# Products of the second half taken chunk by chunk for both column halves, the reciprocal moved by one pair, scratch buffers per batch, SBUF buffers at one common offset

## The chip, the cores and the metric

The program runs on one core of one Trainium2 chip. The metric is device time in microseconds (us); three timed runs of the kernel before gave 576.07 (median), 576.04 and 576.54. A separate, profiled execution gave the trace that is read below; it took 574.43 us, of which 572.6 us are the span from its first to its last instruction.

## The reference, cut to what matters

Attention over 4 batches x 8 heads (576 positions, 64 channels) with rotated q and k, then a gated unit with a mixing matrix over positions, then a causal convolution gate with two more matrix products:

```python
attn = softmax(rot(q) @ rot(k).T / 8) @ v                 # (4, 8, 576, 64), heads side by side: x (4, 576, 512)
h = gelu_tanh(x @ w_in)                                   # 512 -> 1024
u, v = h[..., :512], h[..., 512:]
v_n = (v - mean(v)) / sqrt(var(v) + 1e-6) * g_ln
v_s = einsum('ts,bsd->btd', w_sg, v_n) + b_sg
x2 = x + (u * v_s) @ w_out
gate = sigmoid(causal_conv5(x2, conv_w))
out = (gate * (x2 @ w_val)) @ w_out2                      # (4, 576, 512)
```

## The kernel before

The kernel records every operation as a task of a planner (`Plan`): an engine, an estimated cost, the keys it reads and writes. `P.order()` lays the tasks out once, by what they depend on and when they are due by those estimates, and the instructions are then written in that order. So each engine runs a fixed list, in order, and an instruction that waits holds up all that stands behind it on its engine. SyncE's list (SP) is nearly all DMA issues, about 350 rows.

**First half, attention.** It works on 16 pairs of heads (4 a batch), one pair after the other. A pair's phase on TensorE (`phase`) is a mix of score products of the next pair for its row maxima (`s_unit`, lines 527 and 535, each followed on VectorE by a maximum `mx` or `mn`, lines 529 and 537, that frees the PSUM buffer) and of this pair's transposed scores (`st_unit`, lines 577 and 585, freed by an exponential on ScalarE, line 590). Then comes the pair's "v stretch": the products with v (`pv_unit`, lines 608 and 618) and the row sums (`sum_unit`, line 644). Meanwhile VectorE turns and splits q and k of a later pair (`prep_high`, line 252) and converts a part of a weight (`job_v`, `wa_half`, lines 302 to 308).

A pair's row sums go their own way to memory. ScalarE copies them to `ss` (line 648), a DMA turns them into 128x9 in `rc` (line 651), VectorE takes the reciprocal (line 653), and a DMA writes it to `r_d` (line 654). The unscaled result goes to `xu_d` (line 626). Later the loads `xs<-xu_d` (line 745) and `rb<-r_d` (line 749, spread over 64 partitions) bring both back for GpSimd to multiply. The last 64 positions of two batches are gathered in `xr` and `rr` by `xr_load` (lines 772 and 777): one such call is three DMAs and covers one pair. Eight calls stand in the phases of pairs 8 to 15 (`job_loads`), eight more in the first batch of the second half.

**Second half.** `part_a(b)` makes, for each batch, units of 12 or 24 matmuls with 512 columns (x by the v half of w_in, line 803; the chunk c=4 is `xr`), four units of 24 with 288 columns (the u half, line 844) and four of 28 (the mixing product, `g_unit`, lines 858 and 861; the last chunk of positions, `t4`, comes in by line 861). After these come `x2_part` (line 927), `val_part` (line 960) and `out_part` (line 989). Every product is a sum over four chunks k of 128 rows and three terms: high x high, high x low, low x high (`three`). A unit owns one of four PSUM buffers, each of two banks, and its result is read as a whole when all its matmuls are done. Within the unit a loop over the two banks is the outer one: all 12 terms for the first column half (or the first 128 positions), then all 12 for the second.

The units' inputs come from the other engines: `vn` (the normalised v) is split into a rounded high part by ScalarE and a low part by GpSimd (line 253), chunk by chunk. The first instruction of the second half on ScalarE that uses memory of the first half, the Gelu of line 809 with its table load, waits until all that touched this memory is done, the DMA `r_d<-rc` of the last pair included.

Of the kernel before, what the change touches and what calls it, by code (L numbers as in the profile page):

```python
# [166 lines left out]
def mixer_kernel(ctx: ExitStack, tc: tile.TileContext, qk, v, vrem, cs, w_in, g_ln, w_sgT, b_sg,  # L167
# [32 lines left out]
    mark = const.tile([128, 1], F32, name="mark")  # L200

# [4 lines left out]
    RB = tiles(const, "rb", 2, [128, 4 + S], F32)  # L206

# [33 lines left out]
    ones_b = [att.tile([128, 32], F32, name=f"ones_b{h}") for h in range(2)]  # L241

# [355 lines left out]
    def pv_unit(i, us):  # L598
# [25 lines left out]
        def st(q):  # L624
            for hf in range(2):
                q.dma_start(out=xu_d[i][:, HALF * hf:HALF * hf + HALF].rearrange("(h d) c -> d h c", h=2),
                            in_=xu[64 * hf:64 * hf + 64])
        dma(290, st, [("xu", j2)], [("xu_d", i)], n=2)

    def sum_unit(i, ps, kps):  # L630
# [22 lines left out]
        add("DVE", 0.25, lambda: nc.vector.reciprocal(rc, rc), w=[("rc", j2)])  # L653
        dma(5, lambda q: q.dma_start(out=r_d[i].rearrange("(p c) -> p c", c=9), in_=rc), [("rc", j2)], [("r_d", i)])
# [10 lines left out]
    def attention():  # L665
# [45 lines left out]
        for i in range(NPAIR):  # L711
# [8 lines left out]
            rot = [P.last_pe]  # L720
            if i + 2 < NPAIR:
# [4 lines left out]
            sum_unit(i, PS[2], ("ps", 2))  # L726

# [11 lines left out]
    def three(n):  # L739

        return [(x, y) for x, y in ((0, 0), (0, 1), (1, 0))][:n]

    def x_load(b, hp, after=()):
        i, y = 4 * b + hp, hp % 2
        dma(290, lambda q: q.dma_start(out=XS[y][:, 4:], in_=xu_d[i]), [("xu_d", i)], [("xs", y)], after=after)

        def ld(q):
            for h in range(2):
                q.dma_start(out=RB[y][64 * h:64 * h + 64, 4:], in_=r_d[i][S * h:S * h + S].partition_broadcast(64))
# [19 lines left out]
    def xr_load(b, part, op=()):  # L769
        m, hp = part  # L770
        i, cc = 4 * (b + m) + hp, slice(64 * m, 64 * m + 64)
        dma(32, lambda q: q.dma_start(out=XR[1].bitcast(F32)[:, hp, cc], in_=xu_d[i][:, 512:576]), [("xu_d", i)],
            [("xr", m, hp)], [*op, *P.readers.get(("XR", "l"), ())])

        def ld(q):
            for h in range(2):
                q.dma_start(out=RR[64 * h:64 * h + 64, hp, cc], in_=r_d[i][S * h + 512:S * h + S].partition_broadcast(64))
        dma(32, ld, [("r_d", i)], [("rr", m, hp)], op, n=2)

    def xr_prep(b, after=()):  # L780

        def f():
            return XR[1].bitcast(F32)
        parts = [(m, hp) for m in range(2) for hp in range(4)]
        tt("P", lambda: RR, f, lambda: RR, ALU.mult, 512, [("xr", *x) for x in parts], [("rr", *x) for x in parts], after)
        keys = [("rr", *x) for x in parts]
        acopy(lambda: XR[0], lambda: RR, 512, keys, [("XR", "h")])
        tt("P", lambda: XR[1], lambda: RR, lambda: XR[0].bitcast(F32), ALU.subtract, 512, [("XR", "h"), *keys],
           [("XR", "l"), *[("xr", *x) for x in parts]])

    def part_a(b):
# [4 lines left out]
        for c0 in (0, 2, 4)[:3 - b % 2]:  # L796
            cs_ = (c0, c0 + 1) if c0 < 4 else (4,)

            def mm(ps, cs_=cs_):
                for y, c in enumerate(cs_):  # L800
                    for k in range(4):
                        for z, (p, q) in enumerate(three(3)):
                            nc.tensor.matmul(ps[:, y], X[p][:, k, 128 * c:128 * c + 128] if c < 4 else XR[p][:, k], Wm[q][:, k, 512:1024], start=k == z == 0,  # L803
                                             stop=k == 3 and z == 2)
# [31 lines left out]
        def u_unit(dd):  # L836
            dc = slice(128 * dd, 128 * dd + 128)

            def mm(ps):
                for hf in range(2):  # L840
                    cols = slice(HALF * hf, HALF * hf + HALF)
                    for k in range(4):
                        for z, (p, q) in enumerate(three(3)):
                            nc.tensor.matmul(ps[:, hf, 0:HALF], Wm[p][:, k, dc], X[q][:, k, cols], start=k == z == 0,  # L844
                                             stop=k == 3 and z == 2)
# [4 lines left out]
        def g_unit(dd):  # L850
            dc = slice(128 * dd, 128 * dd + 128)

            def mm(ps):
                for hf in range(2):
                    cols = slice(HALF * hf, HALF * hf + HALF)
                    for k in range(4):
                        for z, (p, q) in enumerate(three(3)):
                            nc.tensor.matmul(ps[:, hf, 0:HALF], VN()[p][:, k, dc], SG[q][:, k, cols], start=k == z == 0,  # L858
                                             stop=False)
# [15 lines left out]
        if b == 0:  # L875
            for x in range(8):
                xr_load(2, divmod(x, 4))
# [32 lines left out]
    def x2_part(b, dds=range(4)):  # L910
        j = b % 2
        for dd in dds:
# [9 lines left out]
            def mm(ps, dc=dc):  # L922
                for hf in range(2):
                    cols = slice(HALF * hf, HALF * hf + HALF)
                    for k in range(4):
                        for z, (p, q) in enumerate(three(3)):
                            nc.tensor.matmul(ps[:, hf, 0:HALF], w2("o", p)[:, k, dc], (T["gh"], T["gl_"])[q][j][:, k, cols],  # L927
                                             start=k == z == 0, stop=k == 3 and z == 2)
# [20 lines left out]
    def val_part(b):  # L949
        j = b % 2  # L950
        rc = slice(64 * j, 64 * j + 64)
        for dd in range(4):
            dc = slice(128 * dd, 128 * dd + 128)

            def mm(ps, dc=dc):
                for hf in range(2):
                    cols = slice(HALF * hf, HALF * hf + HALF)
                    for k in range(4):
# [174 lines left out]
```

## Time and profile before

| | |
|---|---|
| timed, median of 3 | 576.07 us |
| profiled execution | 574.43 us |
| its span, first to last instruction | 572.6 us |
| TensorE busy | 558.7 us, 98% |
| VectorE, ScalarE, GpSimd busy | 70%, 48%, 42% |
| DMA engines' mean share | 45% |

The profile gives busy time by engine, 40 slices of the span, a chain of work that ended last, and timelines by engine. Matmuls overlap one another, so that "busy" of TensorE says only that something was under way. What one matmul costs the stream is the distance from its start to that of the next; over a long run of one kind this is the run's length in the chain divided by its count. Granted clock is 1.00 (2.4 GHz) from 24 us on.

### The profile page before, as it was taken

The numbers are of one execution on the slowest core, as the hardware profiler recorded it, in microseconds if no ns is written. First come the engines' busy times: TensorE is split into PE (matmuls) and PEld (weight loads), VectorE is DVE, ScalarE is ACT, GpSimd is POOL, SyncE is SP. The second block draws the span as 40 slices with busy tenths as digits, with TensorE's granted clock in tenths as the row PEclk, the third lists the DMA queues.
The fourth block names the chain that finished last, engine by engine and source line by source line (L and its number), as shares of the span: only waits on it lengthen the run. The fifth ranks groups of instructions, "written<-read, shape, count | busy, mean of one in ns | idle before, by whom it ended". The sixth has DMA issues, their size and how long they took to land.

```text
span 572.6 us, 12028 instructions
## 1 busy us (share of the span) xinstructions
PE 558.7 (98%) x4658; PEld 466.5 (81%) x4658; DVE 400.8 (70%) x616; ACT 276.7 (48%) x448; POOL 241.3 (42%) x220
## 2 busy tenths in 40 slices
PE   6999999999999999999999999999999999999996
PEld 4677777777777776768999989989999999899985
DVE  4678888888888878534667866645779997647720
ACT  2457666666666666533614426315337443333311
POOL 5534545454545444642876778546410010121100
PEclk9699999999999999999999999999999999999999
DMA  5446747475655565475267481462423341210002
GB/s 211 127 125 191 192 128 204 137 190 130 183 164 150 172 193 153 117 196 138 54 187 259 141 285 58 140 183 73 164 79 112 119 137 42 78 56 1 38 37 92
DMA packets 58697, 77.84 MB, mean 136 GB/s; under 512 B 29968, under 2 KB 34576, under 8 KB 58640
## 3 DMA queue, kind: packets, MB, share of 16 engines
q1 hardware_dynamic: 58496, 77.08, 45.2%
q8 instruction: 36, 0.59, 0.4%
q14 instruction: 21, 0.17, 0.1%
q10 hardware_dynamic: 144, 0.00, 0.0%
HBM read 56.38 MB, written 18.95 MB: 132 GB/s over the span
## 4 chain that ended last, share of the span: by engine, by line
PE 80%; DVE 6%; DMA 6%; ACT 3%; POOL 2%; SPq 2%; issue 1%; POOLq 0%; ACTq 0%; DVEq 0%
PE ps L577 11%; PE ps L608 10%; PE ps L960 9%; PE ps L927 9%; PE ps L989 9%; PE ps L858 6%; PE ps L644 5%; PE ps L527 5%; PE ps L844 4%; PE ps L803 4%; PE ps L585 3%; PE ps L618 2%; PE ps L861 1%; DMA xs<-xu_d 1%; DVE raw L252 1%
## 5 line engine op out<-in xcount | busy, mean ns | idle before, releaser
L529 DVE TENSOR_REDUCE mx<-ps 128x2 f32<-128x576 f32 x128 | 91.4, 753 | 34.1 <-ACT e L590 18.8
L590 ACT ACTIVATE e<-ps 128x576 f32<-128x576 f32 x144 | 85.6, 652 | 30.5 <-PE ps L585 20.3
L608 PE MATMUL ps<-e,vm 128*64 128x288 f32 x512 | 65.6, 409 | 0.0
L858 PE MATMUL ps<-s_h,vn 128*128 128x288 f32 x256 | 56.3, 296 | 1.1 <-POOL vn L253 1.1
L608 PEld LDWEIGHTS ps<-e,vm 128*64 128x64 f32 x512 | 35.3, 137 | 24.7 <-issue 2.6
L253 POOL TENSOR_TENSOR ac<-e,e 128x576 f32<-128x576 f32 x32 | 45.0, 1427 | 7.0 <-ACT e L590 6.8
L252 DVE TENSOR_TENSOR raw<-raw,cst 128x1152 f32<-128x1152 f32 (+2 forms) x35 | 41.6, 1196 | 6.3 <-DMA cst<-cs 6.3
L527 PE MATMUL ps<-kh,qp 64*128 64x288 f32 x256 | 40.4, 346 | 4.1 <-ACT kh L256 1.8
L858 PEld LDWEIGHTS ps<-s_h,vn 128*128 128x128 f32 x256 | 42.8, 188 | 1.3 <-POOL vn L253 1.3
L527 PEld LDWEIGHTS ps<-kh,qp 64*128 64x128 f32 x256 | 23.3, 188 | 19.2 <-issue 8.2
L577 PE MATMUL ps<-mr,one_r 64*128 64x288 f32 x256 | 38.1, 291 | 0.3 <-DMA mr<-mn 0.3
L577 PE MATMUL ps<-qh,kh 64*128 64x288 f32 x256 | 38.2, 293 | 0.0
L577 PE MATMUL ps<-ql,kh 64*128 64x288 f32 x256 | 38.0, 292 | 0.0
L577 PE MATMUL ps<-qh,kl 64*128 64x288 f32 x256 | 38.0, 292 | 0.0
L960 PE MATMUL ps<-xh,wl_v 128*128 128x288 f32 x128 | 37.8, 296 | 0.0
L960 PE MATMUL ps<-xl,wh_v 128*128 128x288 f32 x128 | 37.8, 296 | 0.0
L960 PE MATMUL ps<-xh,wh_v 128*128 128x288 f32 x128 | 37.8, 295 | 0.0
L260 POOL COPY mark<-wf 1x1 f32<-1x1 f32 x12 | 2.1, 174 | 84.8 <-DVE wf L308 84.8
L844 PE MATMUL ps<-XH,w_l 128*128 128x288 f32 x128 | 37.7, 295 | 0.0
L858 PE MATMUL ps<-s_l,vn 128*128 128x288 f32 x128 | 37.7, 295 | 0.0
L844 PE MATMUL ps<-XL,w_h 128*128 128x288 f32 x128 | 37.7, 294 | 0.0
L844 PE MATMUL ps<-XH,w_h 128*128 128x288 f32 x128 | 37.7, 294 | 0.0
(168 smaller groups left out, 1590.0 us busy)
## 6 DMA issues: line engine op xcount, KB each, us to landing
raw<-qk SPq DMA_DIRECT2D x31, 576.0 KB
xu_d<-xu SPq DMA_DIRECT2D x32, 144.0 KB
rb<-r_d SPq DMA_DIRECT2D x32, 144.0 KB
xs<-xu_d SPq DMA_DIRECT2D x16, 288.0 KB
x_d<-xs SPq DMA_DIRECT2D x16, 288.0 KB
g_d<-vs SPq DMA_DIRECT2D x16, 288.0 KB
vm<-v SPq DMA_DIRECT2D x16, 256.0 KB
wr<-w_in SPq DMA_DIRECT2D x8, 512.0 KB
```

Source lines behind the costliest of these rows:

```text
L252: return add("DVE", dve(n), lambda: nc.vector.tensor_tensor(out_(), a(), b(), op), r, w, after, lock=True)
L253: return add("Pool", pool(n), lambda: nc.gpsimd.tensor_tensor(out_(), a(), b(), op), r, w, after, lock=True)
L527: nc.tensor.matmul(ps[:, h, 0:HALF], QP[j2][rows, c], kh[rows, cols], start=True, stop=True)
L529: add("DVE", 0.72, lambda: nc.vector.tensor_reduce(out=MX[j2][:, hk, :, c], in_=ps[:, :, 0:HALF], axis=AX.X, op=ALU.max), [kps], [("mx", j ...
L577: nc.tensor.matmul(ps[:, h, 0:HALF], x[rows, keys] if o < 3 else x[rows], y[rows, cols], start=o == 0, stop=o == 3)
L590: add("Act", 0.62, lambda: nc.scalar.activation(E[n], ps[:, :, 0:HALF], AF.Exp), [kps], [("e", n)])
L608: nc.tensor.matmul(pv[64 * hf:64 * hf + 64, h, 0:HALF], VM[j2][:, j, h], E[EU[i, us[hf]]][:, h], start=j == 0, stop=False, skip_group_chec ...
L844: nc.tensor.matmul(ps[:, hf, 0:HALF], Wm[p][:, k, dc], X[q][:, k, cols], start=k == z == 0, stop=k == 3 and z == 2)
L858: nc.tensor.matmul(ps[:, hf, 0:HALF], VN()[p][:, k, dc], SG[q][:, k, cols], start=k == z == 0, stop=False)
L927: nc.tensor.matmul(ps[:, hf, 0:HALF], w2("o", p)[:, k, dc], (T["gh"], T["gl_"])[q][j][:, k, cols], start=k == z == 0, stop=k == 3 and z == 2)
L960: nc.tensor.matmul(ps[:, hf, 0:HALF], w2("v", p)[:, k, dc], (T["xh2"], T["xl2"])[q][j][:, k, cols], start=k == z == 0, stop=k == 3 and z == 2)
L989: nc.tensor.matmul(ps[:, y], lhs, w2("q", q)[:, k], start=k == z == 0, stop=k == 3 and z == 2)
```

## The change

Five things are changed.

1. `product` replaces the loops of lines 803, 844, 858, 927, 960 and 989. The loop over the two banks (y) is now the innermost: each chunk and term is done for both column halves (or both blocks of 128 positions) before the next. The number of matmuls is the same. In the mixing product the four matmuls with `t4` come after all 24 others.
2. The reciprocal and the write to `r_d` leave `sum_unit` and become `sum_end`, called one pair later, with dependencies that place it after that pair's phase.
3. `xu_d` and `r_d` are one DRAM buffer a batch in place of one a pair, so that `xr_load` brings a batch's four pairs with three DMAs. There are four such calls (12 DMAs) where there were sixteen (48).
4. Three unused tiles (`pad0`, `pad1`, `pad2`) and the move of `mark` to the attention's pool shift the SBUF addresses. The start addresses in the two built programs, modulo 256 bytes:

| tiles | before | after |
|---|---|---|
| XH, XL | 128 | 224 |
| w_h, w_l, s_h, s_l, xr | 0 | 224 |
| vn, t4 | 32 | 224 |
| wh_o to wl_q, gh0, gl0 | 224 | 224 |
| xh2, xl2, yh, yl, yr | 0 | 224 |
| q, k, e and all others of the attention | 96 | 64 |

5. What follows from the planner: other orders on SP and a few exchanges on ScalarE and GpSimd near the end of the attention.

```diff
-    xu_d = [dram.tile([128, S], F32, name=f"xu_d{i}") for i in range(NPAIR)]
+    xu_d = [dram.tile([HP, 128, S], F32, name=f"xu_d{b}") for b in range(B)]
-    r_d = [dram.tile([2 * S], F32, name=f"r_d{i}") for i in range(NPAIR)]
+    r_d = [dram.tile([HP, 2 * S], F32, name=f"r_d{b}") for b in range(B)]
...
-        if i >= 8:
-            xr_load(0, divmod(i - 8, 4), [mq[i]])
+        if i in (8, 10):
+            xr_load(0, i // 2 - 4, [mq[i]])
...
         dma(5, rows, [("ss", 0)], [("rc", j2)])
-        add("DVE", 0.25, lambda: nc.vector.reciprocal(rc, rc), w=[("rc", j2)])
-        dma(5, lambda q: q.dma_start(out=r_d[i].rearrange("(p c) -> p c", c=9), in_=rc), [("rc", j2)], [("r_d", i)])
+
+    def sum_end(i, after=()):
+        rc = RC[i % 2]
+        add("DVE", 0.25, lambda: nc.vector.reciprocal(rc, rc), w=[("rc", i % 2)], after=after)
+        dma(5, lambda q: q.dma_start(out=r_d[i // HP][i % HP].rearrange("(p c) -> p c", c=9), in_=rc), [("rc", i % 2)], [("r_d", i)])
...
             rot = [P.last_pe]
+            if i:
+                sum_end(i - 1, [*rot, *P.writer.get(("mn", (i + 1) % 2, 1), ())] if i + 1 < NPAIR else ())
...
+        sum_end(NPAIR - 1)
...
-    def three(n):
-
-        return [(x, y) for x, y in ((0, 0), (0, 1), (1, 0))][:n]
+    def product(n, out_, lhs, rhs, ends=True):
+
+        terms = [(k, p, q) for k in range(4) for p, q in ((0, 0), (0, 1), (1, 0))]
+        for z, (k, p, q) in enumerate(terms):
+            for y in range(n):
+                nc.tensor.matmul(out_(y), lhs(p, k, y), rhs(q, k, y), start=not z, stop=ends and z == len(terms) - 1)
...
-                for hf in range(2):
-                    cols = slice(HALF * hf, HALF * hf + HALF)
-                    for k in range(4):
-                        for z, (p, q) in enumerate(three(3)):
-                            nc.tensor.matmul(ps[:, hf, 0:HALF], Wm[p][:, k, dc], X[q][:, k, cols], start=k == z == 0,
-                                             stop=k == 3 and z == 2)
+                product(2, lambda y: ps[:, y, 0:HALF], lambda p, k, y: Wm[p][:, k, dc], lambda q, k, y: halves_of(X[q][:, k], y))
...
+                product(2, lambda y: ps[:, y, 0:HALF], lambda p, k, y: VN()[p][:, k, dc], lambda q, k, y: halves_of(SG[q][:, k], y), False)
                 for hf in range(2):
                     cols = slice(HALF * hf, HALF * hf + HALF)
-                    for k in range(4):
-                        for z, (p, q) in enumerate(three(3)):
-                            nc.tensor.matmul(ps[:, hf, 0:HALF], VN()[p][:, k, dc], SG[q][:, k, cols], start=k == z == 0,
-                                             stop=False)
                     for z in range(2):
                         nc.tensor.matmul(ps[:, hf, 0:HALF], T4()[b % 2][:, dc], SG[z][:, 4, cols], start=False, stop=z == 1)
```

VectorE in the phase of pair 12 and the v stretch that follows, before (`mx` are the maxima that free the score buffers `ps`, `wf` the end of a weight's conversion):

```order
L529 TENSOR_REDUCE mx_177<-ps_121 128x2
L653 RECIPROCAL rc_199<-rc_199 128x9
L529 TENSOR_REDUCE mx_177<-ps_123 128x2
L529 TENSOR_REDUCE mx_177<-ps_124 128x2
L529 TENSOR_REDUCE mx_177<-ps_122 128x2
```

The same engine where the reciprocal stands now, at the end of the v stretch:

```order
L308 SCALAR_TENSOR_TENSOR wt_179<-wr_177,wt_179 128x256
L310 SCALAR_TENSOR_TENSOR wf_178<-wr_177,wt_179 128x256
L658 RECIPROCAL rc_175<-rc_175 128x9
L531 TENSOR_REDUCE mx_154<-ps_97 128x2
L531 TENSOR_REDUCE mx_154<-ps_98 128x2
```

The reciprocal has moved from between the fourth and the fifth maximum of a phase to ahead of the first, and it is now that of the pair before.

SP from the small weights to the last `r_d<-rc`, before (`rr<-r_d` are the calls of line 777, `cwr` the convolution's weights):

```order
L362 DMA cwr<-conv_w 128x40
L745 DMA xs_135<-xu_d_74 128x576
L777 DMA rr<-r_d_109 64x64 x2
L626 DMA xu_d_84<-xu_196 64x2x288 x2
L777 DMA rr<-r_d_110 64x64 x2
L651 DMA rc_199<-ss_197 128x1x9
L777 DMA rr<-r_d_111 64x64 x2
L777 DMA rr<-r_d_112 64x64 x2
L755 DMA x_d_89<-xs_134 128x576
L654 DMA r_d_116<-rc_199 128x9
```

SP at the same place now, from the last `xu_d` to the last `r_d<-rc`:

```order
L628 DMA xu_d_72<-xu_173 64x2x288 x2
L653 DMA rc_176<-ss_174 128x1x9
L769 DMA x_d_77<-xs_110 128x576
L763 DMA rb_112<-r_d_90 64x576 x2
L769 DMA x_d_78<-xs_111 128x576
L659 DMA r_d_92<-rc_176 128x9
```

The load of `cwr` is no longer in this piece: it now goes out ahead of the results and sums of the last pair but one (in before, after them). Between the last `rc<-ss` and the last `r_d<-rc` two `rb` loads stand in place of four `rr` loads; both stores of `xs` (`x_d<-xs`) must now be issued first.

## Rows read from the trace of the kernel before

**Rows 1.** The page's first part: busy us, share of span, instructions by engine.

```profile
PE 558.7 (98%) x4658; PEld 466.5 (81%) x4658; DVE 400.8 (70%) x616; ACT 276.7 (48%) x448; POOL 241.3 (42%) x220
```

**Rows 2.** Chain that ended last: start us, length us, what; four row-sum runs.

```profile
107.35 2.08 PE ps L644 x32
...
121.57 2.08 PE ps L644 x32
...
192.69 2.08 PE ps L644 x32
...
223.18 2.08 PE ps L644 x32
```

**Rows 3.** Timeline of VectorE, pair 13: start, length, what, [idle before <-releaser].

```profile
209.59 1.42 DVE L529 TENSOR_REDUCE mx<-ps 128x2 f32<-128x576 f32 x2 [0.74 <-ACT w_h L256]
...
215.69 0.21 DVE L653 RECIPROCAL rc<-rc 128x9 f32<-128x9 f32 x1 [1.63 <-DMA rc<-ss]
215.82 2.70 DVE L529 TENSOR_REDUCE mx<-ps 128x2 f32<-128x576 f32 x4
```

**Rows 4.** Timeline of TensorE, the same stretch.

```profile
214.75 0.71 PE L527 MATMUL ps<-kh,qp 64*128 64x288 f32 x4
216.59 0.40 PE L527 MATMUL ps<-kh,qp 64*128 64x288 f32 x2 [1.13 <-DMA krh<-kh]
```

**Rows 5.** Timeline of SP, the same stretch: DMA issues, start and length.

```profile
209.46 1.16 SPq L777 DMA_DIRECT2D rr<-r_d  x2
210.66 0.58 SPq L772 DMA_DIRECT2D xr_l<-xu_d  x1
...
213.67 0.62 SPq L651 DMA_DIRECT2D rc<-ss  x1
```

**Rows 6.** Timeline of TensorE, first mixing units of batches 0 and 1.

```profile
280.20 0.36 PE L858 MATMUL ps<-s_h,vn 128*128 128x288 f32 x1
281.39 0.40 PE L861 MATMUL ps<-s_h,t 128*128 128x288 f32 x1 [0.83 <-POOL t L253]
...
319.95 0.29 PE L858 MATMUL ps<-s_l,vn 128*128 128x288 f32 x1
321.31 0.40 PE L858 MATMUL ps<-s_h,vn 128*128 128x288 f32 x1 [1.07 <-POOL vn L253]
```

**Rows 7.** Timeline of ScalarE, end of the attention and first Gelu.

```profile
256.89 0.22 ACT L312 ACTIVATE cwt<-cwr 128x20 f32<-128x20 f32 x1 [5.14 <-DMA cwr<-conv_w]
257.01 0.39 ACT L648 ACTIVATE ss<-ps 128x288 f32<-128x288 f32 x1
264.90 1.28 ACT L809 ACT_TABLE_LOAD   x1 [7.50 <-PE ps L803]
266.20 1.94 ACT L809 ACTIVATE gl<-ps 128x1024 f32<-128x1024 f32 x2
```

**Rows 8.** Timeline of SP, the same stretch.

```profile
251.25 0.82 SPq L362 DMA_DIRECT2D cwr<-conv_w  x1
...
257.74 0.60 SPq L651 DMA_DIRECT2D rc<-ss  x1
...
261.51 0.38 SPq L654 DMA_DIRECT2D r_d<-rc  x1
```

**Rows 9.** Chain that ended last: runs of matmuls without a gap.

```profile
218.24 0.26 PE ps L535 x2
...
334.96 13.87 PE ps L803 x60
...
376.39 11.15 PE ps L803 x48
387.54 12.72 PE ps L844 x96
...
453.42 11.20 PE ps L989 x48
...
470.98 12.80 PE ps L960 x96
```

More of the change, by code (lines that the diff above doesn't have):

```diff
@@ L625, in st @@
             for hf in range(2):
[L626 removed]
+                q.dma_start(out=xu_d[i // HP][i % HP, :, HALF * hf:HALF * hf + HALF].rearrange("(h d) c -> d h c", h=2),
                             in_=xu[64 * hf:64 * hf + 64])
@@ L767, in x_prep, with xr_load @@
                 f(b, hp)
[L769 to L773, printed above, removed]
+    def xr_load(b, m, op=()):
+        pairs, cc = range(HP * (b + m), HP * (b + m + 1)), slice(64 * m, 64 * m + 64)
+        dma(128, lambda q: q.dma_start(out=XR[1].bitcast(F32)[:, :, cc], in_=xu_d[b + m][:, :, 512:576].rearrange("h p c -> p h c")),
+            [("xu_d", i) for i in pairs], [("xr", m)], [*op, *P.readers.get(("XR", "l"), ())])
         def ld(q):
             for h in range(2):
-                q.dma_start(out=RR[64 * h:64 * h + 64, hp, cc], in_=r_d[i][S * h + 512:S * h + S].partition_broadcast(64))
-        dma(32, ld, [("r_d", i)], [("rr", m, hp)], op, n=2)
+                q.dma_start(out=RR[64 * h:64 * h + 64, :, cc], in_=r_d[b + m][:, S * h + 512:S * h + S].partition_broadcast(64))
+        dma(128, ld, [("r_d", i) for i in pairs], [("rr", m)], op, n=2)
     def xr_prep(b, after=()):
@@ L799, in mm @@
             def mm(ps, cs_=cs_):
-                for y, c in enumerate(cs_):
-                    for k in range(4):
-                        for z, (p, q) in enumerate(three(3)):
-                            nc.tensor.matmul(ps[:, y], X[p][:, k, 128 * c:128 * c + 128] if c < 4 else XR[p][:, k], Wm[q][:, k, 512:1024], start=k == z == 0,
-                                             stop=k == 3 and z == 2)
+                product(len(cs_), lambda y: ps[:, y],
+                        lambda p, k, y: X[p][:, k, 128 * cs_[y]:128 * cs_[y] + 128] if cs_[y] < 4 else XR[p][:, k],
+                        lambda q, k, y: Wm[q][:, k, 512:1024])
             ps, kp = unit(12 * 0.233 * len(cs_), mm, [*(xk if c0 < 4 else [("XR", m) for m in hl]), *[(f"win{k}_1", m) for k in range(4) for m in hl]])
@@ L875, in part_a @@
         if b == 0:
-            for x in range(8):
-                xr_load(2, divmod(x, 4))
+            for m in range(2):
+                xr_load(2, m)
             xr_prep(2)
@@ L922, in mm @@
             def mm(ps, dc=dc):
[L923 to L928, printed above, removed]
+                product(2, lambda y: ps[:, y, 0:HALF], lambda p, k, y: w2("o", p)[:, k, dc],
+                        lambda q, k, y: halves_of((T["gh"], T["gl_"])[q][j][:, k], y))
             ps, kp = unit(24 * PASS, mm, [gk(j, k, m) for k in range(4) for m in "hl"] + [(f"wo{k}", m) for k in range(4) for m in "hl"])
@@ L955, in mm @@
             def mm(ps, dc=dc):
-                for hf in range(2):
-                    cols = slice(HALF * hf, HALF * hf + HALF)
-                    for k in range(4):
-                        for z, (p, q) in enumerate(three(3)):
-                            nc.tensor.matmul(ps[:, hf, 0:HALF], w2("v", p)[:, k, dc], (T["xh2"], T["xl2"])[q][j][:, k, cols],
-                                             start=k == z == 0, stop=k == 3 and z == 2)
+                product(2, lambda y: ps[:, y, 0:HALF], lambda p, k, y: w2("v", p)[:, k, dc],
+                        lambda q, k, y: halves_of((T["xh2"], T["xl2"])[q][j][:, k], y))
             ps, kp = unit(24 * PASS, mm, [("X2", j, k, m) for k in range(4) for m in "hl"] + [(f"wv{k}", m) for k in range(4) for m in "hl"])
@@ L984, in mm @@
             def mm(ps, cs_=cs_):
-                for y, c in enumerate(cs_):
-                    for k in range(4):
-                        for z, (p, q) in enumerate(three(3)):
-                            lhs = (T["yh"], T["yl"])[p][j][:, k, 128 * c:128 * c + 128] if c < 4 else T["yr"][p][:, b // 2, k]
-                            nc.tensor.matmul(ps[:, y], lhs, w2("q", q)[:, k], start=k == z == 0, stop=k == 3 and z == 2)
+                product(len(cs_), lambda y: ps[:, y],
+                        lambda p, k, y: (T["yh"], T["yl"])[p][j][:, k, 128 * cs_[y]:128 * cs_[y] + 128] if cs_[y] < 4 else T["yr"][p][:, b // 2, k],
+                        lambda q, k, y: w2("q", q)[:, k])
             rk = [("Y", j, k, m) for k in range(4) for m in "hl"] if c0 < 4 else \
```

21 lines of the change are left out of this document (11 added, 10 removed).

## The prediction

> **What bounds the kernel now.** I read the page first. TensorE is busy for 98% of the span and no other engine for more than 70% [rows 1], so the time is TensorE's own stream and the places where it stands still. In the chain of waits the attention repeats exactly. The row sums of one pair start 14.22 us after those of the pair before (107.35 to 121.57), and this chain is nearly all matmuls. Between 192.69 and 223.18 it does not repeat: two pairs take 30.49 in place of 28.44, 2.05 lost [rows 2]. The timeline of TensorE in the second half shows two more holes, at 280.20 and 319.95 [rows 6]; behind them it runs on without a gap, so there a matmul's spacing is the time. A run's length by its count gives it: 12.72/96 = 132.5 ns for 288 columns, 11.15/48 = 232.3 ns for 512 [rows 9]. So the change has two ways to act: fill three holes, or alter the spacing of some 2,000 matmuls.
>
> **The reciprocal.** In the phase of pair 13 VectorE waited 1.63 us for the sums `rc<-ss` before a reciprocal of 0.21, with four score maxima queued behind it [rows 3]. These free the PSUM buffers. TensorE's next score product began at 216.59, just as the first of the four maxima (from 215.82, 2.70 for four) was through [rows 3, 4]. That row names the DMA `krh` as releaser. I read it as the same stall, since the 527 product doesn't use `krh`, but the 585 product behind it does, so an early buffer alone would not be enough. `krh` was late for the same reason as the sums: SP was working through a backlog. There the merging counts. A pair's `rr` and `xr` loads take 1.16 + 0.58 = 1.74 us of SP just ahead of the sums [rows 5]; six of the eight phases that had them lose them, pair 13's among them. With SP 1.7 earlier, both the sums and `krh` come in time. The reciprocal itself now runs at the end of a v stretch, on sums issued a pair earlier, so nothing waits. Its 0.21 us there lie in the idle time before the next pair's first maximum, 0.74 in the one shown [rows 3]; if that cover were gone, it would cost at most 0.21 in each of 14 pairs, 2.9 us. `r_d` is written a pair later, which only the last pairs could feel. Bounds for this part: a loss of 2.9 to a gain of 2.05. I take a gain of 2.0, since the regular pairs show the cover and the price of the irregular one is known.
>
> **The merged loads.** Besides SP's time nothing is gained: the pieces and bytes are the same. 36 issues go in all, half of them in the first batch of the second half, ahead of the first load of w_out. The cost of loading four pairs at once is that it waits for the fourth; the calls at pairs 8 and 10 ask for pairs 0 to 7, which are long done. I cost it at nothing.
>
> **The two holes.** At 280.20 the first mixing unit has done its first column half and waits for `t4`'s low part: 281.39 - 280.20 - 0.13 = 1.06 us. At 319.95 the next batch's first unit waits for the low part of its last chunk: 321.31 - 319.95 - 0.13 = 1.23 us [rows 6]. In the new order `t4` is asked for after 24 matmuls, not after 12: 12 x 0.1325 = 1.59 us later, more than 1.06. The last chunk's low part comes as 23rd, not as 12th: 11 x 0.1325 = 1.46 us later. That would be more than 1.23, but TensorE now also comes there 1.06 sooner, so 1.23 + 1.06 - 1.46 = 0.83 would stay if GpSimd's chain stood still. It should move. The whole chain of the other engines begins with the first Gelu (table load at 264.90), 3.4 us after the issue of the last `r_d<-rc` at 261.51 [rows 7, 8]. The table load's row names TensorE as releaser, but the unit that it reads, 24 x 0.232 = 5.6 us of matmuls behind the last sums, was long done. The program has it wait for that DMA. The DMA in turn was late since the copy of the last sums (257.01) stood on ScalarE behind `cwt`, which had waited 5.14 for `cwr`, issued only at 251.25 [rows 7, 8]. Now `cwr` is issued ahead of the last-but-one pair's sums. Up to 5.1 us of delay go there; SP's new order, where the last `r_d<-rc` stands behind two stores of `xs`, may take some of it back. The part needed is 0.83. I take both holes as closed, 1.06 + 1.23 = 2.3; bounds 1.46 (only the order helps) and 2.5 (with the slower restart behind each). Behind 335 us TensorE would arrive about 4.5 sooner than now, and the later stages' inputs hang mostly on TensorE's own units, so I put no new wait there.
>
> **The spacing.** Two things change it, and no row shows them together. First the order: each stationary block is now followed by the other column half in the other bank. The nearest row is the remainder's score product, one stationary block with two halves into two banks: 0.26 for two, 130 ns [rows 9]. By that, 1,536 matmuls would gain 2.5 ns, 3.8 us. The other bound is a loss: the slowest run of the same size has 12.80/96 = 133.3, so 0.8 ns x 1,536 = 1.2 us. Second the addresses, where stationary and moving operands now all start at 224 modulo 256. Before, the unit of `xr` by w_h was the only 512-column one with equal remainders, and the run of 60 that holds it is 13.87 - 11.15 = 2.72 us longer than that of 48: 226.7 ns for each of these twelve, against 232.3 [rows 9]. If that is the address, 192 matmuls of line 803 gain 5.6 and 216 of line 989 (11.20/48 = 233.3) gain 6.6: 1.1 + 1.4 = 2.5 us. Line 960, with unequal remainders, may come from 133.3 to 132.5: 0.3. From twelve matmuls in a differently built unit I do not take it all. Between a gain of 6.6 and a loss of 1.2, I take 1.5, nearest to the present rows. The attention's buffers shift together, so nothing moves between them.
>
> The Trainium skill says more: "TensorE: Matmul & The Clock Gate", section "Back-to-back issue gap", gives a warm isolated gap of N/2.4 + 2.5 ns, 122.5 for 288 columns and 215.8 for 512. The trace disagrees by 10 and 16.5 ns. If operand placement were the whole of that, then 1,600 x 10 + 432 x 16.5 = 23 us would be to be had and the time were about 548.8; that is a rival of its own, at 3%.
>
> **Sum.** 2.0 + 2.3 + 1.5 = 5.8 us. Against the profiled execution's 574.43 this is 568.6 (a span of 566.8). The profiled execution lies 1.64 below the median of the timed runs; I carry the difference over: 576.07 - 5.8 = 570.3.
>
> **Rivals.** (a) The spacing gains much more. Mechanism: shared stationary block and equal remainders add up, some 4 ns on each 288-column matmul and 6 on each of 512: 6.4 + 2.6 = 9.0 in place of 1.5, time 562.8. For it: the 130 and 226.7 above. Against: in the old order two terms in a row already share a block, in runs that stay at 132.5. (b) The change doesn't do what it says: the holes move. SP's order holds the last `r_d<-rc`, GpSimd comes later, TensorE waits again at the mixing units, or the attention's irregular pair stays since `krh` is still late. Then about 2 of the 4.3 come through and the spacing is flat: 574. Against it: 1.7 us of SP are freed and two separate covers lie over each hole. (c) Slower: alternating banks costs the stream. Mechanism: each matmul adds to a bank that the last one did not write, in all of the second half's 1,920 alternating matmuls. It decides from 4.3/1,920 = 2.2 ns each; at 4 ns, three times the distance between the fastest and the slowest run [rows 9], the loss is 7.7 and the time 579.5. For it: nothing tells what a mixture of 128-row blocks does over a long run. Against: the 130 ns of line 535.
>
> **How the numbers follow.** Forecast, 567 to 573.5: 0.64. Rival (a) 0.12, the page's rule 0.03, rival (b) 0.11, rival (c) 0.10. A measurement of this kernel tells about 0.2% (1.2 us) from no change. Faster: forecast, (a), the rule and about half of (b), 0.84. Same: the other half of (b) and a little of (c), 0.07. Slower: 0.09. The range from 564.5 to 574.2 holds the forecast, most of (b) and some of (a), and leaves out some 0.2.
>
> **What would show it.** After: all pairs at 14.22 between row sums, no reciprocal with idle time in front of it but the one behind the attention; the first Gelu some us earlier against the last row sums; no wait of TensorE on line 253; `cwt` no longer idle for 5 us. The spacing: runs of 288 columns at 131.5 to 132.5, of 512 at 227 to 232. If TensorE waits on `krh` or `mr` in the attention, my reading of SP's backlog is wrong; if the runs come out over 133.5, the forecast of the spacing is, and with 135 the change loses.

## The result and the profile after

The changed kernel takes 567.95 us (median of 6 runs, 567.09 to 568.83); the kernel before, run beside it, 576.31 (573.14 to 578.21). The ratio is 0.9856, 95% interval 0.9827 to 0.9885: about 8.4 us less, and 570.3 was predicted. The profiled execution took 568.26 us, 6.2 less than that of before, with a span of 566.1. The kernel before scatters by 4 to 7 us within a comparison, and in the three later ones its medians were 574.06, 574.92 and 573.86; against those the changed kernel, which was not run beside them, would be 6 to 7 us faster. So the parts are read from the traces. Stretches without a wait repeat there from run to run (pairs at 14.2 us). The waits do not: two later runs whose engines have the same lists as before lose 3.2 us in the attention, not 2.05. What is said of the waits of before holds for its one execution.

The page's first part of the profile after; it answers [rows 1]:

```profile
PE 554.1 (98%) x4658; PEld 467.3 (83%) x4658; DVE 404.1 (71%) x616; ACT 277.0 (49%) x448; POOL 241.3 (43%) x220
```

TensorE still sets the time. In the chain that ended last (start, length, what) the row sums of the pairs around 13 answer [rows 2]:

```profile
107.86 2.08 PE ps L646 x32
...
122.08 2.08 PE ps L646 x32
...
193.21 2.08 PE ps L646 x32
...
207.44 2.08 PE ps L646 x32
...
221.65 2.08 PE ps L646 x32
```

193.21 to 221.65 is 28.44: two regular pairs, where before lost 2.05. The timeline of VectorE in pair 13's phase, for [rows 3]:

```profile
208.79 0.42 DVE L310 SCALAR_TENSOR_TENSOR wf<-wr,wt 128x256 int32<-128x256 int32 x1
209.13 0.21 DVE L658 RECIPROCAL rc<-rc 128x9 f32<-128x9 f32 x1
209.96 1.43 DVE L531 TENSOR_REDUCE mx<-ps 128x2 f32<-128x576 f32 x2 [0.62 <-ACT w_h L258]
```

The reciprocal has no idle time ahead, and 0.62 us of idle time follow it. TensorE at the place of [rows 4] runs on, with the krh product right behind:

```profile
214.48 0.95 PE L529 MATMUL ps<-kh,qp 64*128 64x288 f32 x6
215.39 0.40 PE L587 MATMUL ps<-qh,krh 128*128 128x288 f32 x1
```

Only the last two reciprocals, behind which no score maximum stands, wait for their sums. The end of the attention on ScalarE and on SP, for [rows 7, 8]:

```profile
244.95 0.21 ACT L314 ACTIVATE cwt<-cwr 128x20 f32<-128x20 f32 x1
...
251.35 0.41 ACT L650 ACTIVATE ss<-ps 128x288 f32<-128x288 f32 x1
258.56 1.28 ACT L819 ACT_TABLE_LOAD   x1 [6.81 <-DMA rb<-r_d]
259.85 1.03 ACT L819 ACTIVATE gl<-ps 128x1024 f32<-128x1024 f32 x1
```
```profile
236.82 0.43 SPq L364 DMA_DIRECT2D cwr<-conv_w  x1
...
251.78 0.58 SPq L653 DMA_DIRECT2D rc<-ss  x1
...
254.80 0.38 SPq L659 DMA_DIRECT2D r_d<-rc  x1
```

`cwr` goes out 14.4 us earlier, `cwt` no longer idles, and the Gelu's table load comes at 258.56, not at 264.90. Counted from the start of the last row sums (248.33, before 249.88) that is 10.2 us in place of 15.0. The second half in the chain, for [rows 6, 9]; all products now have one line, L752, but for those with `t4`, L863:

```profile
250.48 29.82 PE ps L752 x180
280.30 0.53 PE ps L863 x4
...
291.94 26.89 PE ps L752 x168
318.82 0.53 PE ps L863 x4
...
410.23 151.42 PE ps L752 x984
```

The first mixing units of batches 0 and 1 are the last 24 matmuls of the runs of 180 and of 168, and their products with `t4` follow at once, at 280.30 and 318.82: both holes are gone. What a matmul costs I worked out from the trace's start times, as the mean distance from one start to the next behind the attention:

| | before | after |
|---|---|---|
| first to last row sums, us | 213.68 | 211.65 |
| first product to last matmul, us | 315.38 | 310.84 |
| waits at `t4` and `vn` in it, us | 1.06 + 1.24 | 0 |
| 512 columns (432 matmuls), ns | 232.7 | 227.1 |
| 288 columns (1,600), ns | 132.8 | 133.0 |

So: attention 2.03, holes 2.30, the first distance behind each hole, 0.24 and not 0.13, some 0.2 together, 512 columns 432 x 5.6 = 2.4 gained, 288 columns some 0.4 lost: the 6.6 that the first two rows give together.

### The profile page after: what moved, and what is told of

Read it like the earlier page. It is cut to its first block, busy times and chain, and to the rows that moved or that the text cites. A ratio compares the mean times of both kernels' runs of the same rounds, so it can differ in the third digit from the quotient of the medians.

```text
span 566.1 us, 11997 instructions
## 1 busy us (share of the span) xinstructions
PE 554.1 (98%) x4658; PEld 467.3 (83%) x4658; DVE 404.1 (71%) x616; ACT 277.0 (49%) x448; POOL 241.3 (43%) x220
## 4 chain that ended last, share of the span: by engine, by line
PE 95%; DVE 2%; DMA 1%; ACT 0%; issue 0%; SPq 0%; ACTq 0%; DVEq 0%
PE ps L752 53%; PE ps L579 12%; PE ps L610 11%; PE ps L646 6%; PE ps L529 5%; PE ps L587 4%; PE ps L620 2%; PE ps L863 2%; DVE mx L531 1%; DVE raw L254 1%; DMA cst<-cs 1%; PE ps L537 1%; ACT qp L258 0%; DVE mn L539 0%; ACT qh L258 0%
## 5 line engine op out<-in xcount | busy, mean ns | idle before, releaser
L254 DVE TENSOR_TENSOR raw<-raw,cst 128x1152 f32<-128x1152 f32 (+2 forms) x35 | 42.8, 1231 | 6.3 <-DMA cst<-cs 6.3
L752 PE MATMUL ps<-s_h,vn 128*128 128x288 f32 x256 | 46.9, 295 | 0.0
L752 PEld LDWEIGHTS ps<-s_h,vn 128*128 128x128 f32 x256 | 38.3, 188 | 0.0
L255 POOL TENSOR_TENSOR vs<-vs,u 128x576 f32<-128x576 f32 x16 | 27.1, 1692 | 26.0 <-DVE vs L867 26.0
L258 ACT CAST qp<-raw 128x512 fp32r<-128x512 f32 x16 | 18.6, 1161 | 35.3 <-DVE raw L254 35.3
L255 POOL TENSOR_TENSOR xl<-xs,xh 128x576 fp32r<-128x576 f32 x4 | 5.9, 1477 | 65.6 <-ACT xh L258 65.6
L943 DVE SCALAR_TENSOR_TENSOR gt<-xs,cw,gt 128x576 f32<-128x576 f32 x32 | 28.2, 884 | 3.8 <-ACT gt L940 3.4
L943 DVE SCALAR_TENSOR_TENSOR gt<-rb,cw,gt 128x576 f32<-128x576 f32 x32 | 28.2, 930 | 3.1 <-ACT gt L940 2.8
L752 PE MATMUL ps<-XL,w_h 128*128 128x288 f32 x128 | 27.4, 296 | 0.0
L752 PE MATMUL ps<-xh,wl_v 128*128 128x288 f32 x128 | 27.4, 296 | 0.0
```

Of the source, the lines that this page charges most:

```text
L254: return add("DVE", dve(n), lambda: nc.vector.tensor_tensor(out_(), a(), b(), op), r, w, after, lock=True)
L255: return add("Pool", pool(n), lambda: nc.gpsimd.tensor_tensor(out_(), a(), b(), op), r, w, after, lock=True)
L258: return add("Act", act(n), lambda: nc.scalar.copy(out_(), in_()), r, w)
L752: nc.tensor.matmul(out_(y), lhs(p, k, y), rhs(q, k, y), start=not z, stop=ends and z == len(terms) - 1)
L943: add("DVE", dve(S) + 0.05, lambda dd=dd, m=m, x2=x2, gt=gt: nc.vector.scalar_tensor_tensor(gt(), x2()[:, m:m + S], cw[:, 5 * dd + m:5 * d ...
```

## The experiments

Each time is the median with its ratio to the kernel before on the same chip. "Products" below is the second row of the table.

**One part alone: the reciprocal.**

```diff
-        add("DVE", 0.25, lambda: nc.vector.reciprocal(rc, rc), w=[("rc", j2)])
+            if i:
+                sum_end(i - 1, [*rot, *P.writer.get(("mn", (i + 1) % 2, 1), ())] if i + 1 < NPAIR else ())
```

> The kernel before with the reciprocal moved and nothing else. Theory as predicted (the maxima behind the reciprocal and the late krh are two effects of one backlog of SP, so the reciprocal alone is not enough): VectorE no longer idles ahead of a reciprocal in pair 13, but TensorE still waits there for krh, and less than half of the 2.05 us is gained. Rival (the reciprocal's wait was the whole stall): all pairs at 14.22 us, 2.0 us gained in the attention. Holes and spacing unchanged in both unless SP's order moves the first Gelu. Time 0 to 1 us under before by the theory, 2 by the rival.

573.98 us, 1.0006 (0.9987 to 1.0026). The two pairs take 14.99 and 14.80, the last 12.88 (before 12.54); first to last row sums is 213.35, 0.33 less than before. SP and TensorE in the phase of pair 13:

```profile
213.58 0.61 SPq L651 DMA_DIRECT2D rc<-ss  x1
214.25 1.12 SPq L428 DMA_DIRECT2D krh<-kh  x2
```
```profile
209.27 0.60 PE L577 MATMUL ps<-mr,one_r 64*128 64x288 f32 x2 [0.33 <-DMA mr<-mn]
...
213.83 0.95 PE L527 MATMUL ps<-kh,qp 64*128 64x288 f32 x6
214.73 0.40 PE L585 MATMUL ps<-qh,krh 128*128 128x288 f32 x1
```

The size is as expected, the reason is not. SP issues the sums and `krh` as late as before (214.25 against 214.34), yet the 527 product has no wait, and the 585 product starts while that issue is still under way: the `krh` it reads is an earlier one. So the 1.13 us of [rows 4] were the buffer held by the maxima behind the reciprocal, and `krh` was not what was late. What is left in the attention are mainly waits for `mr<-mn`, another DMA of the same queue. That wait is not new; TensorE in the kernel before, same phase:

```profile
210.25 0.55 PE L577 MATMUL ps<-mr,one_r 64*128 64x288 f32 x2 [0.26 <-DMA mr<-mn]
```

Set beside the same pairs of the run with merged loads, matmul by matmul, the pairs of before lose about 0.15 us one phase earlier, 0.65 around this wait and 1.25 at that of [rows 4].

The second half got worse in this execution: products 318.15, 2.8 more than before. TensorE waits four times there, 0.21 and 0.82 us in the first mixing unit of batch 0 and twice in that of batch 1:

```profile
319.54 0.53 PE L864 MATMUL ps<-s_h,vn 128*128 128x288 f32 x2 [0.62 <-POOL vn L253]
...
321.28 0.40 PE L864 MATMUL ps<-s_h,vn 128*128 128x288 f32 x1 [1.08 <-POOL vn L253]
```

Behind these two waits the granted clock is 0.50 (1.2 GHz) from 321.7 to 325.1 us, and products of 288 columns start 240 ns apart: some 1.5 us more. In the trace of before the clock stays at 1.00 behind its holes. The execution took 576.03, 2.05 over the kernel's median, so one trace does not say how often this happens.

**One part alone: the merged loads** (with one DRAM buffer a batch and the new `xr_load`).

```diff
-        if i >= 8:
-            xr_load(0, divmod(i - 8, 4), [mq[i]])
+        if i in (8, 10):
+            xr_load(0, i // 2 - 4, [mq[i]])
```

> The kernel before with one DRAM buffer a batch and the merged loads, nothing else. Theory as predicted (SP's backlog makes both the sums and krh late): with 1.7 us of SP freed in pair 13's phase the sums come in time although the reciprocal stands where it stood, all pairs at 14.22 us, 2.0 us gained, and the conversion weights' load goes out earlier, so that the first Gelu starts up to 5 us earlier and the holes shrink. Rival (the backlog has another source): VectorE idles over 1 us ahead of the reciprocal in pair 13 still, the pair stays irregular, nothing gained. Spacing unchanged in both.

569.60 us, 0.9923 (0.9906 to 0.9939): 4.4 us. Every pair is at 14.21 to 14.23, products 312.87, no wait over 0.2 us in them. SP, VectorE and ScalarE, with the reciprocal where it was:

```profile
210.72 0.62 SPq L651 DMA_DIRECT2D rc<-ss  x1
211.39 1.13 SPq L428 DMA_DIRECT2D krh<-kh  x2
```
```profile
213.85 0.21 DVE L653 RECIPROCAL rc<-rc 128x9 f32<-128x9 f32 x1
214.36 2.09 DVE L529 TENSOR_REDUCE mx<-ps 128x2 f32<-128x576 f32 x3 [0.30 <-ACT e L590]
```
```profile
245.11 0.21 ACT L312 ACTIVATE cwt<-cwr 128x20 f32<-128x20 f32 x1
...
258.56 1.28 ACT L807 ACT_TABLE_LOAD   x1 [6.79 <-DMA rb<-r_d]
```

The sums are issued 3 us earlier (210.72, [rows 5] 213.67), the reciprocal waits for nothing, the table load stands at 258.56 as in the changed kernel. This part alone ends all three stalls. In every run with merged loads the planner also puts `cwr` ahead of the sums of the last pair but one (here at 236.22); no run moves that one load alone, so whether its place would be enough for the two holes is open.

**Which of the merged calls.** The calls of the second half one pair at a time again, on the merged buffers:

```diff
-            for m in range(2):
-                xr_load(2, m)
+            for x in range(8):
+                xr_load_one(2, *divmod(x, 4))
```

> The kernel before with one buffer a batch, merged loads for the calls in the attention, and the eight calls of the first batch of the second half pair by pair as before. Theory (SP's time in the attention's phases is the cause): all pairs at 14.22 us, the load of cwr ahead of the last-but-one pair's sums, first Gelu near 259 to 261, no wait on t4 or vn, 4 us under before, as with all loads merged. Rival (the calls of the second half, issued ahead of the last write to r_d, make the first Gelu late): the pairs regular (2 us gained), first Gelu over 262 and a wait on t4 or vn left, 2 to 3 us under before.

569.93 us, 0.9923 (0.9901 to 0.9945); products 312.87, no wait; ScalarE:

```profile
258.40 1.28 ACT L818 ACT_TABLE_LOAD   x1 [6.67 <-DMA r_d<-rc]
```

The last `r_d<-rc` does go out later here (256.41, in the fully merged run 254.82), and the table load is named as waiting for it, but it comes no later. The 18 issues taken out of the attention, with what the planner moves for them, carry the whole gain.

**One part alone: the order of the products.**

```diff
-                for hf in range(2):
-                    cols = slice(HALF * hf, HALF * hf + HALF)
-                    for k in range(4):
-                        for z, (p, q) in enumerate(three(3)):
+        for z, (k, p, q) in enumerate(terms):
+            for y in range(n):
```

> The kernel before with the new order of the products alone, addresses, reciprocal and loads as before. Theory: the holes at t4 and vn shrink to 0 and under 0.9 us, 1.4 to 2.3 us gained; 512 columns stay at 232 to 233 ns; 288 columns show 131 ns with one interval of about 140 or 136 in every two or four, mean 132 to 133.5, no gain. The irregular attention pair stays. Time 1.4 to 2.3 us under before, ratio 0.996 to 0.9975. Rival (the order makes the 227 ns): 512 columns at 227 and 2.4 us more. Rival (the 140 ns come from the addresses): 288 columns at a plain 131 to 132, 1 to 2 us more.

572.72 us, 0.9988 (0.9966 to 1.001). Products 314.23. 512 columns stay at 233.0 ns, 288 come to 133.1. No wait at `t4`; at `vn` one is left, 0.57 us over a matmul:

```profile
321.71 0.53 PE L744 MATMUL ps<-s_h,vn 128*128 128x288 f32 x2 [0.41 <-POOL vn L253]
```

So the order covers what it was said to cover, and gives part of it back in spacing: the products gain 1.15 us of the expected 1.4 to 2.3. In the time none of it is clear of noise, since the interval holds 1. The attention, its lists those of before, keeps its waits: the two pairs take 15.20 and 16.41 in this execution (before 14.37 and 16.12).

**One part alone: the addresses.**

```diff
-    mark = const.tile([128, 1], F32, name="mark")
+    const.tile([128, 32], F32, name="pad0")
+    const.tile([128, 96], F32, name="pad1")
+        pa2.tile([128, 80], F32, name="pad2")
```

> The kernel before with the three pads and the moved tile alone; order of instructions unchanged. Theory (the 512-column spacing comes from equal remainders modulo 256): the 512-column matmuls go from 232 to 233 ns to 227 ns, 432 x 5.6 ns = 2.4 us gained; the 288-column ones keep 132.5 with no intervals of 140 ns, which belong to the order; the irregular attention pair and the two holes (1.06 at t4, 1.23 at vn) stay or change by what TensorE now does earlier. Time 2.4 us under before, ratio 0.996. Rival (the spacing comes from the two banks in turn): 512 columns stay at 232 to 233 and the time stays within 0.2%. Rival (the 140 ns come from the addresses): they show here.

573.05 us, 0.9966 (0.9946 to 0.9986). Runs in the chain, for [rows 9] (L805 is 803 there, L991 is 989, L962 is 960):

```profile
334.28 13.64 PE ps L805 x60
...
375.49 10.90 PE ps L805 x48
386.39 12.72 PE ps L846 x96
...
452.12 10.90 PE ps L991 x48
...
469.38 12.72 PE ps L962 x96
```

10.90/48 = 227.1 ns for 512 columns in all these runs, 12.72/96 = 132.5 for 288, also on line 960. The instructions and their order are those of before, so the addresses alone make the 5.6 ns. The hole at `t4` happened to close; that at `vn` stayed (1.24), and the pairs are irregular.

**The loads unmerged again, the rest as changed.**

```diff
-        if i in (8, 10):
-            xr_load(0, i // 2 - 4, [mq[i]])
+        if i >= 8:
+            xr_load(0, divmod(i - 8, 4), [mq[i]])
```

> The changed kernel with one buffer a pair and the unmerged loads again; reciprocal, order of the products and addresses as changed. Theory after the first four runs (the merged loads alone end all three stalls, the rest adds the 512-column spacing): the attention has its irregular pairs again (some 2 us), the first Gelu comes near 264 as in the kernel before, the t4 hole stays covered by the order, a part of the vn hole (0.5 to 0.9) stays: 2 to 3.5 us over the changed kernel, so 2.5 to 4 under before; 512 columns at 227 ns. Rival (my prediction's joint covers: reciprocal and order would have closed them without the merging): the time of the changed kernel within 0.5 us.

571.91 us, 0.9946 (0.9922 to 0.9969). The span is 569.9, 3.8 us over the changed kernel's, a little more than expected, though its first row sums start 1.4 us sooner; from there to the last matmul it is 4.9 over, 2.7 in the attention and 2.2 behind it. The late table load, and TensorE's waits in the first mixing unit of batch 1:

```profile
264.20 1.28 ACT L821 ACT_TABLE_LOAD   x1 [7.46 <-DMA r_d<-rc]
```
```profile
320.00 0.80 PE L752 MATMUL ps<-s_h,vn 128*128 128x288 f32 x4 [0.68 <-POOL vn L255]
321.75 0.52 PE L752 MATMUL ps<-s_h,vn 128*128 128x288 f32 x2 [0.69 <-POOL vn L255]
```

Three pairs are late, by 0.58, 0.91 and 1.24. Reciprocal and order don't replace the merging.

**The old loop order back, the rest as changed.**

```diff
-        for z, (k, p, q) in enumerate(terms):
-            for y in range(n):
+        for y in range(n):
+            for z, (k, p, q) in enumerate(terms):
```

> The changed kernel with the column half (or block of positions) as the outer loop again in all products, the rest as changed. Theory (the new order is worth nothing once the loads are merged and costs the intervals of 140 ns): 288 columns at a mean of 132.5 as with the addresses alone, no interval at 140, 512 columns at 227, no hole at t4 or vn: 0.5 to 0.8 us under the changed kernel. Rival (the order covers holes that would show here): PE waits for t4 or vn of 0.5 to 2 us, and the time is over the changed kernel's.

566.32 us, 0.9860 (0.9834 to 0.9886). Products 309.97, 0.87 less than in the changed kernel; no wait. The last run of products in the chain, to set beside 151.42:

```profile
408.82 150.82 PE ps L752 x984
```

288 columns come to 132.5 ns. The ratios of the two kernels to before (0.9860, 0.9856) don't separate them; the two traces show the order as a loss of 0.5 ns a matmul.

**Loads and addresses alone,** reciprocal and order as before; the edit is the sum of the two diffs above.

> The kernel before with the merged loads and the addresses only: reciprocal and order of the products as before. Theory (two of the four parts carry the whole result): 288 columns at 132.5, 512 at 227, all pairs at 14.22, no hole: the time of the run with the outer loop back, 566.3, within 0.5 us, so some 8 us under before and 1.5 under the changed kernel. Rival (the moved reciprocal is worth something by itself): VectorE waits ahead of a reciprocal by over 0.5 us in some pair, and the time is 0.5 to 2 us over 566.3.

566.94 us, 0.9870 (0.9847 to 0.9892); all pairs 14.21 to 14.24, products 310.03, no wait. It lies 0.6 us over the run before it, with overlapping intervals. Two of the four parts carry the result.

**Other remainders.**

```diff
-    const.tile([128, 96], F32, name="pad1")
+    const.tile([128, 128], F32, name="pad1")
+    pA.tile([128, 48], F32, name="pad3")
+        p2.tile([128, 48], F32, name="pad4")
+        p2.tile([128, 56], F32, name="pad5")
```

> The changed kernel with other pads, so that the stationary block and the moving operand of the 512-column products start apart, modulo 256: XH by w_h 128, xr by w_h 192, y by wh_q 64, yr by wh_q 32. Theory (only equal remainders give 227 ns): all four at 229 to 234 ns. Rival (multiples of 64 are as good as 0): the first three at 227, yr alone at 233. Rival (the order of the products gave the 227): all at 227. The 288-column products of w_v and of the u half and the mixing product also have unequal starts here (128 apart), those of gh0 by wh_o equal ones; by the address theory they come out 0.3 to 0.8 ns longer than in the changed kernel.

569.17 us in one execution, products 312.29. 512 columns, means of the runs behind the first: XH by w_h 232.2 to 232.3 ns, `xr` by w_h 230.3, y by wh_q 233.0 to 233.3, `yr` by wh_q 232.9 to 233.1. None is at 227. The expectation for 288 columns failed: their mean is 132.5, 0.6 under the changed kernel. The trace shows why: the u half's units of batches 0 and 2 take 132 and 128 ns in turn, 130.0 on average, those of batches 1 and 3 mostly 131 three times and then 140, 133.1 on average, with the same SBUF addresses and the same order inside the unit. So the halves in turn have a second, cheaper pattern, and address and order of a unit alone don't decide which one comes.

**Halves in a snake.**

```diff
-            for y in range(n):
+            for y in (range(n) if z % 2 == 0 else reversed(range(n))):
```

> The changed kernel with the order of the two halves reversed in every second term (0 1 1 0 0 1 1 0), so that no matmul goes from the second half of one term back to the first half of the next. Theory A (the 140 and 136 ns belong to that step back): all 288-column intervals at 131 to 132, 2 ns x 1,600 = 3 us under the changed kernel. Theory B (a set number of ns falls on every four matmuls whatever the step): mean stays 132 to 133.3, time unchanged. 512 columns at 227 in both.

570.05 us, 0.9916 (0.9890 to 0.9941), products 312.72. Neither theory: 288 columns rise to 134.1 ns.

**Parts of 256 and 320 columns,** with the outer loop and with the inner one.

```diff
-        return x[..., HALF * y:HALF * y + HALF]
+        return x[..., 256:S] if y else x[..., 0:256]
+    def out_of(ps, y):
+        return ps[:, 1, 0:S - 256] if y else ps[:, 0, 256:512]
```

> The run with the outer loop back, its 288-column halves replaced by 256 and 320 columns, so that the second part of the moving operand also starts at the stationary block's remainder modulo 256 (1,024 bytes further, not 1,152); in PSUM the two parts lie end to end over the bank's border. In the run with 288 columns the u half's units show 131.2 ns in the first column half (equal remainders) and 133.1 in the second (128 apart). Theory: each pair of 256 and 320 columns costs 2 x 131.3 = 262.6 in place of 264.5 to 265 ns, 800 pairs x 2 = 1.6 us under 566.3. Rival (a matmul of 256 columns meets a floor, such as its weight load): 256 columns at over 125 ns where their share would be 118, 4 us or more over 566.3.

> The changed kernel (column halves in turn) with 256 and 320 columns in place of twice 288. Theory A (the 140 ns of the changed order come from the second half's unequal start): no interval stands out at 9 ns over its own size, a pair costs 262.6 as in the run with the outer loop, 2.7 us under the changed kernel. Theory B (they belong to changing the bank or the half at every matmul): some intervals still 5 to 9 ns over the others of their size, the pair at 265 to 267, no gain.

567.60 us, 0.9894 (0.9869 to 0.9920), and 567.96, 0.9899 (0.9875 to 0.9923); products 311.30 and 311.31. Mean distances in the first and the second set of twelve, or the first and the second of two in turn, of the u half's units, in ns:

| kernel | one part | the other | mean |
|---|---|---|---|
| before (128 apart, equal) | 133.5 | 131.6 | 132.5 |
| addresses alone (equal, 128 apart) | 131.5 | 133.4 | 132.4 |
| changed (in turn) | 131.3 | 135.1 | 133.2 |
| 256 and 320, outer loop (both equal) | 119.7 | 146.9 | 133.3 |
| 256 and 320, in turn (both equal) | 117.4 | 149.1 | 133.3 |

The first two lines show the address once more: the column half with equal starts is the cheaper one by 1.9 ns, and it changes sides with the pads. In the changed order every second distance is 131.3 on average and the others 135.1: most are 131, but every fourth is 140. (With the order alone, on the old addresses, some units have 135 in every second place.) With parts that both start equal, nothing stands out by 9 ns, as theory A had it, but the pair costs 266.6 ns, not 262.6: the 256 columns take 13.0 ns over 256/2.4 and the 320 take 13.6 over 320/2.4, where 288 with equal starts take 11.5 over. No floor of 125 either. Both prices that I had set were wrong, and why 288 columns cost less over their length stays open.

## Why the prediction was right, and where it was not

**The bound and the three stalls: right in size.** The attention was to give 2.0 and gave 2.03; the two holes 2.3 and gave 2.30. That the sizes agree so closely is luck in part: they are those of one trace of before, and with the same lists the attention lost 3.2 in two later executions, and the hole at `t4` did not come in one.

**The attention: the wrong share.** The step "an early buffer alone would not be enough. `krh` was late" fell: with the reciprocal alone `krh` goes out as late as before and TensorE doesn't wait for it. A releaser's name in [rows 4] was read as a second cause, though the sentence before had found that the instruction doesn't use it. But the reciprocal alone was still not enough (0.33 of 2.03 gained), for another reason: TensorE also waits for `mr`, another DMA of the same queue. That wait was in the trace of before, at 210.25, with about 0.65 of the 2.05, and the prediction had no term for it. "With SP 1.7 earlier, both come in time" is the part that held, and it needs no moved reciprocal. The cover over the reciprocal's new place held too: where a maximum follows it, 0.55 to 0.67 us of idle time are left between the two, 0.15 in the first pair, and all pairs are at 14.22.

**The holes: two covers, and one is the cause.** I counted the order and the earlier first Gelu together. The second came by 4.8 us of at most 5.1, and it closes both holes without the order. The order by itself closes `t4` and leaves 0.57 of `vn`, near the 0.83 given for GpSimd's chain standing still. The merging was costed at nothing besides SP's time; what SP's shorter list does was all of it, 4.4 of the 8 us.

The Trainium skill ("DMA: Bandwidth & Descriptors", section "Issuing engines are not separate DMA queues") calls the time that a sequencer takes to initiate a DMA usually small relative to the DMA itself. One by one the trace of before agrees for a long DMA (`xs<-xu_d` at 250.30: an issue of 0.43 us, 6.19 until the chain goes on) and hardly for a short one (`rc<-ss` at 244.33: 0.62 of 1.92). Summed on one queue it doesn't, since 18 issues less in the attention are worth 4.4 us.

**The spacing: net 2.0 against 1.5, from two mis-sized terms.** The addresses gave the full 2.4 us on 512 columns (2.5 was the bound) and 0.5 on 288; I took part of it since only twelve matmuls stood behind it. The order, bounded by a gain of 3.8 and a loss of 1.2, lost 0.9 (the changed kernel against its outer loop). The 130 ns of line 535, two halves of one block, come back in only one of the four mixing units of each batch (130.1); over all 1,600 the mean is 133.0. That a gain of 2.9 and a loss of 0.9, neither of them sized alone in the forecast, come out near 1.5 together is luck. So "runs of 288 columns at 131.5 to 132.5" was wrong, and "of 512 at 227 to 232" right at its lower end. Rival (c) had the sign for 288 columns, at a seventh of its 4 ns (which is five times the 0.8 between the rows of 288 columns, not three). Rival (a), 562.8, fell with the same number.

The isolated gap that the Trainium skill gives ("TensorE: Matmul & The Clock Gate", section "Back-to-back issue gap"), 2.5 ns over N/2.4, isn't reached by any kind of product of the second half: 512 columns with equal starts are 13.8 over, 288 at least 10 (the units at 130). The 548.8 of that rival is out by 19 us.

**The sum and the median.** Against the profiled execution the sum gave 568.6 and 568.26 came. Of the 2.35 us between 570.3 and 567.95, 1.95 are the 1.64 that I carried over from before: its three runs lay above the profiled one, while the median of after lies 0.3 below its own. In the later comparisons the kernel before had medians of 573.9 to 574.9. The offset was the scatter of three runs and belonged in the range.

## What to carry to other kernels

When one queue issues nearly all DMAs back to back, count the issues that can go from it before looking at the instructions that wait: three stalls of TensorE, which came by way of VectorE, ScalarE and GpSimd, had one cause, and 18 issues less, with the order that the planner then chose, removed them all. A releaser's name is a lead; ask whether the instruction uses it. Where two covers lie over one hole, change one at a time, since the one not needed may be paying for itself elsewhere.

## What the runs showed of the hardware that was not expected

A 512-column fp32r matmul takes 227 ns from start to start where the stationary block and the moving operand start at the same byte modulo 256, and 230 to 233 ns on average at the distances tried (32, 64, 128 and 192); for 288 columns in the old order it is 131.5 against 133.4 in the u half, though parts of 256 and 320 columns, both with equal starts, gained nothing. For 512 columns the equality counts, not the place: 0 and 0 in the kernel before ([rows 9], 226.7) and 224 and 224 in the changed one give the same. But what ran before counts too: with the same equal starts, the first unit of `xr` in the kernel before (at 263.3) has distances of 224 to 236 ns until its last four, which are at 227, a mean of 229.9. Two column halves in turn give patterns of 131 ns with 140 in every fourth or 135 in every second place, or of 132 and 128, which is 130 on average; two and two (the snake) give a mean of 134.1. Which mechanism makes these wasn't settled. Waits cost more than their length where the clock falls behind them: with the reciprocal alone, two waits of 0.62 and 1.08 us within 2 us were followed by 3.4 us at a granted clock of 0.50. The Trainium skill ("TensorE: Matmul & The Clock Gate", section "Step-by-step: what each phase is for") has the streaming operand and the weight load on separate read ports of SBUF, so that they don't take bandwidth from each other; the start addresses, by which these 5.6 ns come and go with no instruction changed, make one ask whether the two share something after all; no run here shows it.
